# Reordering a chunked RWKV7 + MLP kernel: corner transpose ahead of an MLP piece, a second N tile, groups in pairs, weight conversions ahead of the third inverse

## The chip, the cores and the metric

One NeuronCore of a Trainium2 chip. The metric is the device time of one execution in microseconds (us). Every kernel was run four times on the chip (one of the runs with the profiler), beside runs of the kernel before on the same chip. Engine names are those of the profile: PE is the matrix engine, PEld its weight loads, DVE the vector engine, ACT the scalar engine, POOL the GpSimd engine, SP the engine that issues the DMAs.

## The reference

An RWKV7 recurrence over 768 steps for 4 batches x 8 heads with head size 40, whose output is fed as 3072 rows of 320 to an MLP with exact gelu.

```python
for t in range(S):                       # S = 768
    y[:, :, t] = einsum('bhd,bhde->bhe', rt, state)
    Sa = einsum('bhde,bhe->bhd', state, at)
    state = state * wt - einsum('bhd,bhe->bhde', Sa, bt) + einsum('bhd,bhe->bhde', vt, kt)
x = y.transpose(0, 2, 1, 3).reshape(B * S, H * D)      # 3072 x 320
h = x @ w_in                                           # 320 x 2048
out = (0.5 * h * (1 + erf(h / sqrt(2)))) @ w_out       # 2048 x 320
```

The MLP's weights arrive as 64-bit floats. The kernel loads their words and makes 32-bit floats of them on the chip.

## The kernel before

The sequence is cut into 12 chunks of 64 steps. Each chunk needs groups of small matmuls on PE (N, RV, A, M, av, X, sap, saT, QY and so on, 64 matmul records each), and the inverse of a triangular block, which is done by column steps on POOL (on DVE for chunk 0). "Corner" and "joined" put two 32-wide inverses together to a 64-wide one. The MLP of a chunk is cut into 8 pieces, four `ph` and four `po`; `fill()` puts one piece into PE's order between groups.

The corner's transpose L is issued where the corner is:

```python
def corner(c):
    t = turned_in[c]
    Tt, _ = inverses[c]
    L = work.tile([P, 2 * G * NP, BL], FP32, tag="L", name="L")
    nc.vector.transpose(L, flat(Tt)[:, :, :BL])
    N = flat(t["N"])
    J = duo("J")[:, 0].rearrange(...)
    for n in range(2 * G * NP):
        for q in range(2):
            mm(J[...], N[lo[q], n, BL:], L[lo[q], n])
    ...
```

The last two of the four `po` pieces end with a copy `os` on DVE, and each `ph` piece ends with a gelu on ACT into `gt`, a tile that also serves as scratch for the raw words of w_in at the start:

```python
def mlp(c):
    xt = xts.pop(c)
    for q in range(NF // 4):
        ph = duo("ph")...                      # 40 matmul records from xt and w_in_sb
        nc.scalar.activation(gt[:, 4 * q:4 * q + 4]..., ph, ACT.Gelu)
        yield
    po = duo("po")[:, :, :DM]
    for part in range(2):
        for g in range(G):                     # 16 matmul records from gt and w_out_sb
            ...
            if part:
                os = work.tile([P, DM], FP32, tag="os", name="os")
                nc.vector.tensor_copy(os, po[:, g])
                ...                            # stores to out
            yield
```

One conversion of words to floats. `convert(n)` advances a queue of these generators, so that the second half of one follows the first half of the next:

```python
def to_float(dst, words, eng):                 # eng: POOL for w_in, DVE for w_out
    ...
    nc.vector.tensor_scalar(power, hi, 0x7FF00000, None, ALU.bitwise_and)
    nc.scalar.activation(power, power, ACT.Relu, bias=rebias, scale=8.0)
    nc.vector.tensor_scalar(mant, hi, 0x000FFFFF, 0x00100000, ALU.bitwise_and, ALU.bitwise_or)
    yield
    nc.vector.scalar_tensor_tensor(power, hi, 0x80000000, power, ALU.bitwise_and, ALU.bitwise_or)
    if eng is nc.vector:
        ...                                    # two more operations on DVE
    else:
        nc.scalar.mul(lo_f, lo, 2.0 ** -52)
        nc.scalar.mul(mant_f, mant, 2.0 ** -20)
        eng.tensor_tensor(mant_f, mant_f, lo_f, ALU.add)
        eng.tensor_tensor(dst, mant_f, power_f, ALU.mult)
    yield
```

The start is laid by hand; on each engine the instructions stand in the order of these calls (one transpose that stood behind a copy on DVE cost 11.6 us in the loop, as b_corner below shows). The part around the third inverse (chunk 2's, on POOL), and the end of the start:

```python
    first_pieces(range(NK), 1, nc.gpsimd)      # the second half of w_in, five conversions
    ...
    make_N(2)
    run(start_inverse(2, nc.gpsimd))
    convert(1)
    fill()
    make_y2(1)
    make_M(1)
    convert(1)
    load_v(2)
    load_r(2)
    turn_k(2)
    convert(1, True)
    second_load(4, 6)
    fill()
    second_pieces((*range(NF - 2), NF - 1, NF - 2), nc.vector)
    seconds(2, (5, 2, spare_raw), (6, 0, spare_raw))
    fill()
    make_QY(1)
    outputs(1)
    ...                                        # w_out's conversions between the groups of chunk 2
```

The loop over chunks 2 to 11, cut to the part that matters:

```python
    for c in range(2, NCH):
        ...
        make_QY(c); outputs(c); pieces.append(mlp(c))
        ...
        if more2:
            turn_b(n + 1)
        fill()                                 # a po piece: its os copy is on DVE
        if more:
            corner(n)                          # L behind that os copy on DVE
        if more2:
            turn_k(n + 1); make_N(n + 1); run(start_inverse(n + 1, nc.gpsimd))
        fill()
        if more:
            joined(n)
```

## Time and profile before

| | before |
|---|---|
| time, median (range) of 4 runs | 843.96 us (840.51 to 844.67) |
| span of the profiled run | 838.1 us |
| start, to the first matmul of X(2) | 254.3 us |
| loop, from X(2) to the end | 583.8 us |
| one chunk of the loop | 56.06 us |

The page cuts the span into 40 slices; a digit is a tenth, and in the row PEclk it is the granted clock of PE. Two rows of the page of the kernel before:

```profile
PE   7236771165669999999999999999999999999997
PEclk8555595575859999999999999999999999999999
```

Up to the 12th slice PE is idle for over a fifth of each slice, in two of them for over four fifths, and often at half clock; after that it is full. So anything that shortens the first 254 us must take away waits, and anything that shortens the rest must take away work or waits of PE itself. The prediction below shows the waits.

### The profile page before, as it was taken

How to read it: one execution, taken by the hardware profiler on the slowest of the kernel's cores; microseconds unless marked ns; L12 is line 12 of the kernel's file. 1: busy time of each engine (PE TensorE's matmuls, PEld its weight loads, DVE VectorE, ACT ScalarE, POOL GpSimd, SP SyncE). 2: the span in 40 equal slices, each digit the busy share in tenths (PEclk: the TensorE clock that was granted, in tenths of full speed). 3: DMA queues.
4: the chain of work that ended last, by engine and by line, in shares of the span. 5: the costliest groups of instructions: out<-in, count | busy, mean ns of one | idle time of the engine just before them, and what ended most of it. 6: DMA issues, size and time to landing. Idle time of an engine off the chain costs nothing.

```text
span 838.1 us, 30219 instructions
## 1 busy us (share of the span) xinstructions
PE 702.7 (84%) x13646; PEld 563.3 (67%) x13646; DVE 279.1 (33%) x422; ACT 214.0 (26%) x260; POOL 315.2 (38%) x781
## 2 busy tenths in 40 slices
PE   7236771165669999999999999999999999999997
PEld 4226661054448878778788787787887877868785
DVE  3763440147542422432424324324233243211000
ACT  5002540212312412422323124223232242111010
POOL 4282336620105507418246074182461751810000
PEclk8555595575859999999999999999999999999999
DMA  9876743017617247354372473543724733020000
GB/s 132 158 156 130 147 112 89 0 40 155 142 34 140 43 82 130 60 103 80 64 135 50 84 135 55 109 77 68 129 57 76 142 55 65 4 53 10 25 9 16
DMA packets 274705, 70.27 MB, mean 84 GB/s; under 512 B 263248, under 2 KB 267856, under 8 KB 274576
## 3 DMA queue, kind: packets, MB, share of 16 engines
q1 hardware_dynamic: 274412, 68.17, 42.6%
q8 instruction: 107, 1.75, 0.9%
q14 instruction: 22, 0.18, 0.1%
q10 hardware_dynamic: 164, 0.16, 0.1%
HBM read 54.13 MB, written 10.22 MB: 77 GB/s over the span
## 4 chain that ended last, share of the span: by engine, by line
PE 73%; POOL 6%; DMA 6%; issue 5%; SPq 4%; DVE 4%; ACT 0%; POOLq 0%; DVEq 0%
PE ph L726 25%; PE po L734 24%; PE QY L100 5%; PE J L100 2%; PE N_ps L100 2%; DMA w_out_sb<-in_moe_w_in_dram 2%; PE cum L100 2%; PE M_ps L100 1%; POOL W L548 1%; POOL mant L281 1%; PE sap L100 1%; POOL tmp L546 1%; PE saT_ps L100 1%; PE X L100 1%; PE wT_ps L100 1%
## 5 line engine op out<-in xcount | busy, mean ns | idle before, releaser
L726 PE MATMUL ph<-xt,w_in_sb 64*128 64x256 f32 x1920 | 225.8, 388 | 42.2 <-ACT gt L728 29.8
L734 PE MATMUL po<-w_out_sb,gt 128*128 128x320 f32 x768 | 225.7, 448 | 9.1 <-DVE w_out_sb L277 8.0
L726 PEld LDWEIGHTS ph<-xt,w_in_sb 64*128 64x128 f32 x1920 | 185.7, 190 | 68.0 <-ACT gt L728 30.2
L734 PEld LDWEIGHTS po<-w_out_sb,gt 128*128 128x128 f32 x768 | 145.9, 195 | 72.2 <-DVE w_out_sb L277 12.4
L546 POOL TENSOR_TENSOR tmp<-W,Nb 128x126 f32<-128x126 f32 (+22 forms) x310 | 111.8, 361 | 213.2 <-DMA Nb<-N 189.7
L548 POOL TENSOR_TENSOR W<-W,tmp 128x126 f32<-128x126 f32 (+22 forms) x310 | 113.9, 368 | 24.3
L728 ACT ACTIVATE gt<-ph 128x1024 f32<-128x1024 f32 x48 | 49.1, 1024 | 232.5 <-PE ph L726 197.5
L738 DVE COPY os<-po 128x320 f32<-128x320 f32 x24 | 11.8, 492 | 152.5 <-PE po L734 152.5
L413 POOL TENSOR_TENSOR ks<-k_raw,part 128x640 f32<-128x640 f32 x10 | 21.2, 2119 | 100.5 <-ACT part L378 85.1
L100 PE MATMUL RV_ps<-rT,vT 40*64 40x64 f32 x768 | 16.4, 244 | 30.8 <-DVE rT L166 30.8
L100 PEld LDWEIGHTS RV_ps<-rT,vT 40*64 40x64 f32 x768 | 14.7, 156 | 34.5 <-issue 34.5
L686 DVE TENSOR_TENSOR xt<-QY,wpT 128x512 f32<-128x512 f32 x24 | 15.5, 686 | 65.5 <-PE QY L100 65.5
L464 DVE TENSOR_TENSOR SM<-M_ps,upper 128x1024 f32<-128x1024 f32 x12 | 14.7, 1224 | 65.7 <-PE M_ps L100 65.7
L464 DVE TENSOR_TENSOR A<-A_ps,upper 128x1024 f32<-128x1024 f32 x12 | 14.7, 1221 | 54.6 <-PE A_ps L100 54.6
L520 ACT COPY avs<-av 128x640 f32<-128x640 f32 x12 | 8.3, 692 | 90.4 <-PE av L100 51.8
L464 DVE TENSOR_TENSOR VR<-RV_ps,upper 128x1024 f32<-128x1024 f32 x12 | 14.7, 1225 | 47.7 <-PE RV_ps L100 47.7
L100 PE MATMUL J<-L,N 32*32 32x32 f32 x768 | 9.9, 204 | 23.9 <-DVE L L585 23.9
L270 ACT ACTIVATE power<-power,rebias 128x320 uint32<-128x320 uint32 (+1 forms) x26 | 16.0, 623 | 51.6 <-DVE power L269 51.6
L100 PEld LDWEIGHTS J<-L,N 32*32 32x32 f32 x768 | 8.9, 116 | 29.4 <-issue 29.4
L464 DVE TENSOR_TENSOR N<-N_ps,upper 128x1024 f32<-128x1024 f32 x12 | 14.7, 1225 | 36.0 <-PE N_ps L100 36.0
L424 DVE TENSOR_TENSOR aT<-aT,wpT 128x1024 f32<-128x1024 f32 x12 | 24.0, 2001 | 1.6 <-ACT wpT L380 0.4
L728 ACT ACT_TABLE_LOAD x10 | 12.8, 1283 | 42.6 <-PE ph L726 40.1
(133 smaller groups left out, 869.0 us busy)
## 6 DMA issues: line engine op xcount, KB each, us to landing
Nb<-N SPq DMA_DIRECT2D x22, 256.0 KB
VR<-in_v_dram SPq DMA_DIRECT2D x24, 160.0 KB
out_dram<-os SPq DMA_DIRECT2D x48, 80.0 KB
w_tile<-in_w_dram SPq DMA_DIRECT2D x22, 160.0 KB
b_raw<-in_b_dram SPq DMA_DIRECT2D x22, 160.0 KB
k_raw<-in_k_dram SPq DMA_DIRECT2D x22, 160.0 KB
v_pairs<-in_v_dram SPq DMA_DIRECT2D x48, 72.0 KB
r_pairs<-in_r_dram SPq DMA_DIRECT2D x48, 72.0 KB
```

The costliest lines, as they stand in the source:

```text
L100: nc.tensor.matmul(o, lhsT, rhs, start=first, stop=True, skip_group_check=True)
L270: nc.scalar.activation(power, power, ACT.Relu, bias=rebias, scale=8.0)
L413: nc.gpsimd.tensor_tensor(ks[:, :, :, :D], raws.pop((c, "k")), rwv, ALU.mult)
L424: nc.vector.tensor_tensor(flat_a, flat_a, wp, ALU.mult)
L464: nc.vector.tensor_tensor(to, pt, upper.unsqueeze(1).to_broadcast([P, 2 * G * NP, C]), ALU.mult)
L546: eng.tensor_tensor(t, W[:, :rows, j:j + 1].to_broadcast([P, rows, rest]), Nb[:, j:j + 1, j + 1:].to_broadcast([P, rows, rest]), ALU.mult)
L548: eng.tensor_tensor(W[:, :rows, j + 1:], W[:, :rows, j + 1:], t, ALU.add)
L686: nc.vector.tensor_tensor(xt[:, :NP, g * P:(g + 1) * P].rearrange("p i (e t) -> p i e t", e=2), Y, wp[:, g, :, :, :C], ALU.mult)
L726: nc.tensor.matmul(ph[:, x, s], w_in_sb[half(x), kt, p * P:(p + 1) * P], xt[half(x), kt], start=kt == 0, stop=kt == NK - 1)
L728: nc.scalar.activation(gt[:, 4 * q:4 * q + 4].rearrange("p (x s) t -> p x s t", x=2), ph, ACT.Gelu)
L734: nc.tensor.matmul(po[:, g], gt[:, f, g * P:(g + 1) * P], w_out_sb[:, f], start=f == 0, stop=f == NF - 1)
L738: nc.vector.tensor_copy(os, po[:, g])
```

## The change

The intent: in the loop, take the corner's transpose out of PE's way, and put two groups of matmuls into each gap between MLP pieces (which needs a second N tile, since N of the chunk after next is now written ahead of the join). In the start, have all of w_in converted ahead of the third inverse, which occupies POOL for 27 us. The core of the diff; other moves of loads and turns are cut.

```diff
@@ to_float
-        yield
+        if eng is nc.vector:
+            yield
@@ make_N
-        N = t["N"] = work.tile([P, 2, G, NP, C], FP32, tag="turned" if c == 1 else "N", name="N")
+        if c > 1 and c % 2:
+            N = work.tile([P, 4 * DM], FP32, tag="spare", name="N")[:, :2 * G * NP * C]
+            N = N.rearrange("p (j g n t) -> p j g n t", j=2, g=G, n=NP)
+        else:
+            N = work.tile([P, 2, G, NP, C], FP32, tag="turned" if c == 1 else "N", name="N")
+        t["N"] = N
@@ corner
+    def turn_corner(c):
+        L = turned_in[c]["L"] = work.tile([P, 2 * G * NP, BL], FP32, tag="L", name="L")
+        nc.vector.transpose(L, flat(inverses[c][0])[:, :, :BL])
@@ start: the third inverse
+    convert(4, True)
     run(start_inverse(2, nc.gpsimd))
-    convert(1)
+    second_load(4, 6)
+    second_load(5, 2, spare_raw)
+    second_load(6, 0, spare_raw)
     fill()
+
+    second_pieces((*range(NF - 2), NF - 1, NF - 2), nc.vector)
     make_y2(1)
     make_M(1)
-    convert(1)
+    seconds(2, (7, 14))
+    fill()
     load_v(2)
     load_r(2)
...
     make_QY(1)
     outputs(1)
+    pieces.append(mlp(1))
+    seconds(2, (8, 12), (9, 10))
     load_VR(3)
...
+    fill()                                 # the fourth ph piece, now behind QY(1)
+    turn_k(2)
     turn_v(2)
     turn_r(2)
     make_RV(2)
...
-    seconds(1, (15, 14))
+    seconds(2, (13, 2, spare_raw))
+    store_inverse(2)                       # stood further up, ahead of scale(3)
+    fetch_inverse(2)
     turn_b(3)
+    seconds(1, (14, 0, spare_raw), (15, 14))
@@ loop
+        corner(c)
         make_X(c)
         fill()
         if more2:
-            load_next(n + 1)
+            load_next(n2)
+        joined(c)
         if more:
             make_RV(n)
+        fill()
         make_sa(c)
-        fill()
         make_saT(c)
-        if more:
-            make_A(n)
         fill()
...
-        fill()
-        if more:
-            corner(n)
-        if more2:
-            turn_k(n + 1)
-            make_N(n + 1)
-            run(start_inverse(n + 1, nc.gpsimd))
+        fill()
+        if more2:
+            make_N(n2)
+            run(start_inverse(n2, nc.gpsimd))
+            turn_k(n2)
+        if more:
+            turn_corner(n)
         fill()
-        if more:
-            joined(n)
```

More of the change, by code (lines that the diff above doesn't have):

```diff
@@ L203 @@
     ahead = {n: t.rearrange("p (g h d) -> p g h d", g=G, h=H) for n, t in ahead.items()}
-    spare_raw = const.tile([P, 4 * DM], UINT32, name="spare_raw")
+    spare_raw = work.tile([P, 4 * DM], UINT32, tag="spare", name="spare_raw")
     early_a = spare_raw.bitcast(FP32).rearrange("p (n d) -> p n d", d=BW)
@@ L578 @@
     hi = [slice(q * HP + BL, (q + 1) * HP) for q in range(2)]
+    def turn_corner(c):
+        L = turned_in[c]["L"] = work.tile([P, 2 * G * NP, BL], FP32, tag="L", name="L")
+        nc.vector.transpose(L, flat(inverses[c][0])[:, :, :BL])
     def corner(c):
         t = turned_in[c]
-        Tt, _ = inverses[c]
-        L = work.tile([P, 2 * G * NP, BL], FP32, tag="L", name="L")
-        nc.vector.transpose(L, flat(Tt)[:, :, :BL])
+        if "L" not in t:
+            turn_corner(c)
+        L = t.pop("L")
         N = flat(t["N"])
@@ L799 @@
     load_VR(0)
-    load_v(0)
     spare_x = work.tile([P, NK, TB], FP32, tag="xt", name="spare_x").rearrange("p k t -> p (k t)")
@@ L807 @@
     run(start_inverse(1, nc.gpsimd, (spare_x[:, :BL * BL], spare_w[:, :nw], spare_w[:, nw:])))
+    load_v(0)
     load_r(0)
@@ L812 @@
     first_load(False, 1)
-    first_load(True, 0, early(4))
     run(inverse)
     store_inverse(0)
+    load_VR(1)
+    fetch_inverse(0)
     turn_v(0)
@@ L821 @@
     turn_k(1)
-    make_A(1, False)
-    load_VR(1)
-    fetch_inverse(0)
-    load_v(1)
-    first_load(False, 2, early(5, 4))
-    first_pieces(range(NK), 0, nc.gpsimd)
-    mask_A(1)
-    corner(0)
+    load_v(1)
+    first_load(True, 0, early(4))
+    first_pieces((0, 1), 0, nc.vector)
+    convert(2)
+    corner(0)
+    make_A(1, False)
     joined(0)
@@ L832 @@
     make_sa(0)
-    convert(1)
+    mask_A(1)
+    first_pieces((2, 3, 4), 0, nc.gpsimd)
+    make_saT(0)
     store_inverse(1)
@@ L836 @@
     load_r(1)
-    load_w(2)
-    make_saT(0)
     convert(1)
-    fetch_inverse(1)
     make_y2(0)
     make_M(0)
-    convert(1)
+    fetch_inverse(1)
+    load_w(2)
     load_a(2)
     load_kb(2)
-    logs(2)
-    first_load(False, 3)
+    convert(1)
     make_QY(0)
@@ L850 @@
     pieces.append(mlp(0))
-    first_load(True, 1, spare_raw[:, :LW])
+    first_load(False, 2, early(5, 4))
     turn_v(1)
@@ L855 @@
     turn_state()
+    first_load(False, 3)
+    first_load(True, 1, spare_raw[:, :LW])
     convert(1)
@@ L860 @@
     make_X(1)
-    convert(1)
+    logs(2)
     first_pieces(range(NK), 1, nc.gpsimd)
@@ L866 @@
     make_sa(1)
-    scale(2)
+    scale_b(2)
     turn_a(2)
     scale_a(2)
-    convert(1)
     make_saT(1)
     turn_b(2)
+    scale_k(2)
+    for f, at in enumerate((14, 12, 10, 8)):
+        second_load(f, at)
     convert(1)
     fill()
-    for f, at in enumerate((14, 12, 10, 8)):
-        second_load(f, at)
     make_N(2)
+    convert(4, True)
     run(start_inverse(2, nc.gpsimd))
-    convert(1)
+    second_load(4, 6)
+    second_load(5, 2, spare_raw)
+    second_load(6, 0, spare_raw)
     fill()
+    second_pieces((*range(NF - 2), NF - 1, NF - 2), nc.vector)
     make_y2(1)
     make_M(1)
-    convert(1)
+    seconds(2, (7, 14))
+    fill()
     load_v(2)
     load_r(2)
-    turn_k(2)
-    convert(1, True)
-    second_load(4, 6)
-    fill()
-    second_pieces((*range(NF - 2), NF - 1, NF - 2), nc.vector)
-    seconds(2, (5, 2, spare_raw), (6, 0, spare_raw))
-    fill()
     make_QY(1)
     outputs(1)
+    pieces.append(mlp(1))
+    seconds(2, (8, 12), (9, 10))
     load_VR(3)
-    pieces.append(mlp(1))
-    seconds(3, (7, 14), (8, 12))
-    load_w(3)
-    load_a(3)
-    load_kb(3)
+    fill()
+    turn_k(2)
     turn_v(2)
@@ L905 @@
     make_A(2)
+    load_w(3)
+    load_a(3)
+    load_kb(3)
+    seconds(3)
+    seconds(2, (10, 2, spare_raw), (11, 0, spare_raw), (12, 14))
+    fill()
     make_av(2)
-    seconds(2, (9, 10))
+    logs(3)
     load_v(3)
     load_r(3)
-    seconds(2, (10, 2, spare_raw), (11, 0, spare_raw))
-    fill()
-    logs(3)
-    seconds(2, (12, 14))
     sums(3)
-    store_inverse(2)
-    fetch_inverse(2)
     scale(3)
@@ L919 @@
     scale_a(3)
-    seconds(2, (13, 2, spare_raw), (14, 0, spare_raw))
+    seconds(2)
     turn_state()
     fill()
-    seconds(1, (15, 14))
+    seconds(2, (13, 2, spare_raw))
+    store_inverse(2)
+    fetch_inverse(2)
     turn_b(3)
+    seconds(1, (14, 0, spare_raw), (15, 14))
     seconds(2, last=True)
     fill()
-    corner(2)
-    turns_b(3)
     make_N(3)
     run(start_inverse(3, nc.gpsimd))
+    turns_b(3)
+    turn_corner(2)
     fill()
-    joined(2)
     for c in range(2, NCH):
-        n = c + 1
-        more, more2 = n < NCH, n + 1 < NCH
+        n, n2 = c + 1, c + 2
+        more, more2 = n < NCH, n2 < NCH
+        corner(c)
         make_X(c)
@@ L939 @@
         if more2:
-            load_next(n + 1)
+            load_next(n2)
+        joined(c)
         if more:
             make_RV(n)
+        fill()
         make_sa(c)
-        fill()
         make_saT(c)
-        if more:
-            make_A(n)
         fill()
@@ L952 @@
         if more2:
-            logs(n + 1)
+            logs(n2)
         make_QY(c)
@@ L956 @@
         pieces.append(mlp(c))
+        fill()
         if more2:
-            load_VR(n + 1)
-            turn_a(n + 1)
-            turn_v(n + 1)
-            turn_r(n + 1)
-        fill()
+            load_VR(n2)
+            sums(n2)
         if more:
-            make_av(n)
+            make_A(n)
+            turn_state()
         if more2:
-            sums(n + 1)
-            scale(n + 1)
-            scale_a(n + 1)
-        if more:
-            turn_state()
+            scale(n2)
+            turn_a(n2)
+            scale_a(n2)
         fill()
@@ L974 @@
             fetch_inverse(n)
+            make_av(n)
         if more2:
-            turn_b(n + 1)
+            turn_b(n2)
+            turn_v(n2)
+            turn_r(n2)
         fill()
+        if more2:
+            make_N(n2)
+            run(start_inverse(n2, nc.gpsimd))
+            turn_k(n2)
         if more:
-            corner(n)
-        if more2:
-            turn_k(n + 1)
-            make_N(n + 1)
-            run(start_inverse(n + 1, nc.gpsimd))
+            turn_corner(n)
         fill()
-        if more:
-            joined(n)
     fill(1000)
```

## The prediction

> **What bounds the kernel now.** I read the page first (its slices show two regimes), then the busy time in stretches, then PE's waits and timeline in each regime, then whatever those waits named.
>
> Busy time by stretches (start:end; us; PE, PEld, DVE, ACT, POOL with instruction counts; PE clock; DMA share; GB/s):
>
> ```profile
> 100.00:125.00 25.00, 19.79 (x375) 16.57 (x377) 10.55 (x17) 14.27 (x20) 9.87 (x10) 0.85 0.40 106
> 125.00:150.00 25.00, 3.47 (x124) 2.93 (x113) 1.23 (x1) 0.00 (x0) 16.36 (x44) 0.56 0.32 74
> 150.00:175.00 25.00, 7.06 (x28) 4.29 (x30) 6.53 (x11) 6.57 (x10) 15.96 (x27) 0.50 0.08 27
> ...
> 325.00:350.00 25.00, 25.00 (x502) 20.39 (x499) 10.85 (x13) 8.57 (x9) 17.55 (x41) 1.00 0.31 61
> 350.00:375.00 25.00, 23.71 (x488) 18.76 (x488) 7.07 (x9) 5.28 (x6) 2.89 (x11) 1.00 0.52 96
> ```
>
> From 254 us to the end PE is full at clock 1.00; one chunk takes 56.06 us (RV starts at 259.98, 316.06, 372.12 in the chain). Every second or third stretch lacks exactly 1.29 us. Before 254 PE is a third to a half idle, often at half clock. So the run is a start of 254 us bound by waits, and a loop of 584 us bound by PE. PE's waits in the start, and then in the loop (total, times, longest):
>
> ```profile
> PE RV_ps L100 <- DVE rT L166: 30.8, 2, 19.7
> PE ph L726 <- ACT gt L728: 29.8, 1, 29.8
> PE ph L726 <- POOL w_in_sb L282: 12.4, 4, 4.1
> ...
> PE po L734 <- DVE w_out_sb L277: 8.0, 6, 2.8
> ```
>
> ```profile
> PE J L100 <- DVE L L585: 11.6, 9, 1.3
> PE po L734 <- DVE os L738: 1.2, 2, 0.6
> ```
>
> *The long wait.* "ACT gt" is only the last link. The timelines of PE, POOL and ACT around it:
>
> ```profile
> 128.00 1.81 PE L388 MATMUL kT_ps<-ident,ks 128*128 128x128 f32 x8 [1.35 <-DVE SM L464]
> 159.61 2.08 PE L726 MATMUL ph<-xt,w_in_sb 64*128 64x256 f32 x8 [29.80 <-ACT gt L728]
> ```
>
> ```profile
> 157.23 1.27 POOL L281 TENSOR_TENSOR mant<-mant,gt 128x512 f32<-128x512 f32 x1
> 158.58 1.27 POOL L282 TENSOR_TENSOR w_in_sb<-mant,power 128x512 f32<-128x512 f32 x1
> ```
>
> ```profile
> 158.54 1.02 ACT L728 ACTIVATE gt<-ph 128x1024 f32<-128x1024 f32 x1 [34.95 <-POOL mant L281]
> ```
>
> The third inverse occupies POOL from 130.27 to 157.2. The conversions of the second half of w_in stand behind it; the second gelu overwrites gt, which still holds their raw words, so it waits too, and PE waits for its bank. POOL then needs until 172.4 for the four conversions left, and ph trickles with them.
>
> *The short wait.* In DVE's order the corner's transpose L stands behind the output copy os, which waits for the end of the po piece just ahead of the corner on PE:
>
> ```profile
> 357.23 0.49 DVE L738 COPY os<-po 128x320 f32<-128x320 f32 x1 [6.22 <-PE po L734]
> 357.64 0.70 DVE L585 STREAM_TRANSPOSE L<-Tt 128x512 f32<-128x512 f32 x1
> ```
>
> 0.49 + 0.70 and two hand-overs make the 1.29 us, nine times.
>
> [...]
> 1. [...]the w_in wait of 4.07 us at 114.30 is followed by 24 matmuls in 4.72 us, where 40 take 4.59 us in the loop.
> 2. [...]L and the gelu above are held by what stands ahead of them.
> 3. [...]a po piece takes 4.50 us start to next start between tiled groups (338.67 to 343.17), 4.31 beside transposes (347.54 to 351.85): about 0.19 us for one stay in the full-array mode.
> 4. [...]the two mask operations of a w_out conversion took 1.39 and 1.42 us at 169.86 while POOL converted, 0.32 each at 187.33 with POOL idle.
>
> **The change part by part.** I laid out each engine's new order with the durations above; starts are in us of the span.
>
> *Loop.* The transpose L goes ahead of the last po piece, so it is done 4 us before PE asks for it; the second N tile only lets the new N be written while the corner still reads the old one. Removed: 9 x 1.29 = 11.6 us. Pairing groups adds and removes no matmul. Full-array stays per chunk fall from five (po; cum; tn-po-nT-po; kT; po) to four (po-cum; tn-po; nT-po; kT-po): 1 x 0.19 x 9 = 1.7 us. Joined(2) moves inside the loop's account: +0.7. Net -12.6 us. New waits I looked for: with two groups and a piece per gap a bank of the four comes back about 4.5 us after its last writer, evictions take 0.4 to 1.3 us; tn needs cum's bank (exp, 0.7 us) two groups later; av needs A's mask a whole piece later. All hidden.
>
> *Start, to the first ph piece: about nothing.* Moving v loads behind the second inverse's load starts that inverse some 3 us sooner on POOL, but slows DVE's inverse beside it; one and a half conversions go to DVE ahead of the first corner (6 or 7 operations, about 4.5 us). L(0) stays near 62.9, the first QY ends near 83 (81.2 before), the second corner near 88 (87.9 before). The first ph piece starts at 108 as before.
>
> *First ph piece: gain 6 us.* Its five w_in conversions are now done by 96, so the 4.07 us wait and the half clock go: end 112.7, not 118.95; M of chunk 1 ends near 120.3, not 126.6.
>
> *The third inverse.* Four conversions remain after N(2). Each is 2.55 us on POOL, fed through DVE and ACT, and with the two buffers of power and mant: POOL runs from 117.4 to about 129.5. The gelu of the second ph piece stands behind the last one on ACT, so the third ph piece gets its bank at about 128 (half clock: 6.5 us, to 134.5). QY(1) ends at 137.5, not 184.3: **47 us earlier**. The inverse itself runs from 129 to 157, as now, but nothing needs it before 178.
>
> *What is given back.* From QY(1) to the loop's first X it was 184.3 to 254.3, 70 us. Now the fourth ph piece stands inside (+4.5); v and r of chunk 2 load only after spare_raw is free (near 130), so RV comes at about 147; the w_out conversions, 1.93 us each (187.33 to 189.25), begin beside the inverse[...]. Five of them (to 162), av, log and cum (168), po (175), then the loads of the last three w_out rows, of which two stand in the queue behind the inverse's store and fetch (about 9 us, as at 216.48 to 224.7): third po piece done near 200; N, kT, po and J (1.9 + 1.9 + 6.3 + 1.0, as after 241.2) put X(2) at about 212. So 74.5 us, not 70: the start gains 254.3 - 212 = **42 us**.
>
> Sum: 844.3 - 42 - 12.6 = 789.7, say **790 us**.
>
> **The rivals.**
> (a) *The start's gain is taken back by the w_out chain.* For: DVE, ACT and the one DMA queue make each w_out row in turn and PE waited 8.0 us for them; the raw rows share few slots. Against: of 70 us there, much was work and waits that simply move. If the loads slip another 15 us: about 805.
> (b) *Only the loop counts*, if some DMA sets the time of QY(1): the second half of w_in is now loaded later, after xt. For: 2 MB at about 160 GB/s take 12.5 us. Against: they land near 106 to 109, and the first is needed at 109. If QY(1) moved only 20 us: about 815.
> (c) *The loop gets a new wait* from the pairing, of 1 us per chunk: about 800. Against: PE's only waits in the loop are those above.
> (d) *The start goes better*: [...]RV earlier: about 778.
>
> **Range and chances.** (a) and (c) are likelier than (d), so 790 already carries some contention; the hand-laid start can be 15 us off either way: 772 to 808. Within 2% would need under 17 us, when the loop alone gives 12 and the POOL block 30: 0.03. Slower needs a stall not seen here: 0.01.
>
> **What would show it.** Right: no PE wait for L in the loop, period near 54.6 us; no PE wait over 10 us between 105 and 140; POOL's third inverse after the last w_in conversion, near 129; QY(1) end near 137; X(2) near 212. Wrong: a period still near 56 or a new wait for a PSUM bank in the loop; the ph wait turned into an equal wait for w_out, v/r or DMA between 137 and 212.

The sum stays as recorded, 844.3 - 42 - 12.6 = 789.7, said as 790 us. Inside the 42 one term is cut: about 3 us, an estimate without a source, that the w_out conversions beside the inverse were to lose. "Five of them (to 162)" contains it. Item 4 has such operations longer beside POOL; why, the traces don't show.

- The 0.19 us for one stay (groups whose matmuls the trace gives as 128\*128, between smaller tiles) is the estimate from the two times in item 3. What costs it is not shown.
- The 6.5 us for a `ph` piece at half clock are an estimate too: the first piece lost 1.97 us (24 matmuls in 4.72 us, where the loop's pace gives 2.75), and 4.59 + 1.97 is 6.56. The clock records have half clock there, from 114.6 to 118.0 us.
- "About 160 GB/s" is an estimate from the page, which has up to 158 GB/s in the first four slices of the kernel before.
- That an inverse on POOL slows the one on DVE: column steps of 128x56 took DVE 0.22 us each at 29.82 and 30.07 with POOL idle, 0.40 and 0.44 at 46.08 and 46.52 with POOL at its own inverse. The cause is not shown.

## The result

| | before | after |
|---|---|---|
| time, median (range) of 4 runs | 843.96 us (840.51 to 844.67) | 805.43 us (801.70 to 806.65) |
| span of the profiled run | 838.1 us | 802.8 us |
| start, to X(2) | 254.3 us | 220.4 us |
| loop, from X(2) to the end | 583.8 us | 582.4 us |

The ratio is 0.9544 (95% interval 0.9501 to 0.9586). Here and below, a ratio is the mean time of one kernel's runs over that of the other's of the same rounds, so not quite the ratio of the medians. The time lies inside the range that was predicted, near its upper end; 15 us are missing from the predicted gain of 54. The table says where: the start gained 34 us and not 42, and the loop hardly gained at all. (The profiled run of the kernel before took 839.78 us, less than the four in the table, so the two profiles differ by 35.3 us and the medians by 38.5.) The same two rows of the page of the kernel after:

```profile
PE   7326675467699999999999999999999999999997
PEclk8555677867699999999999999999999999999999
```

**The start.** Busy time by stretches of the kernel after, with the columns that the prediction explains:

```profile
100.00:125.00 25.00, 19.54 (x416) 16.22 (x418) 9.92 (x14) 11.56 (x16) 5.98 (x5) 0.83 0.71 171
125.00:150.00 25.00, 16.54 (x288) 14.27 (x280) 13.11 (x17) 6.88 (x10) 21.29 (x40) 0.80 0.48 115
150.00:175.00 25.00, 10.32 (x142) 6.49 (x142) 21.81 (x44) 5.75 (x9) 12.93 (x33) 0.69 0.66 139
...
550.00:575.00 25.00, 23.82 (x582) 20.65 (x580) 4.79 (x5) 6.25 (x8) 17.23 (x46) 0.93 0.69 130
```

Between 125 and 150 us PE now works 16.5 us, where it worked 3.5: the block behind the third inverse is gone. From 150 on DVE is the full engine (21.8 of 25 us); it converts w_out. The last row is in the loop, where PE should be full at clock 1.00, and is not. PE's waits in the first 240 us of the kernel after, largest first:

```profile
PE RV_ps L100 <- DVE rT L166: 31.6, 2, 21.0
PE po L745 <- DVE w_out_sb L278: 16.0, 9, 6.9
...
PE ph L737 <- POOL mant L282: 8.3, 1, 8.3
PE saT_ps L100 <- issue: 5.5, 1, 5.5
```

The 29.8 us for the gelu have become 8.3. The wait for w_out doubled, from 8.0 to 16.0. And 5.5 us are put down to "issue", that is, to nothing the profile shows. These lines of PE's timeline place them (start, length, what, count, and in brackets the idle time ahead of it):

```profile
109.16 1.44 PE L100 MATMUL saT_ps<-Tt,part 64*64 64x64 f32 x38 [5.46 <-issue]
...
112.43 5.99 PE L737 MATMUL ph<-xt,w_in_sb 64*128 64x256 f32 x40
118.34 1.16 PE L100 MATMUL N_ps<-aT,nT 40*64 40x64 f32 x64
...
134.39 6.94 PE L737 MATMUL ph<-xt,w_in_sb 64*128 64x256 f32 x40 [8.35 <-POOL mant L282]
...
160.49 1.99 PE L100 MATMUL RV_ps<-rT,vT 40*64 40x64 f32 x64 [10.61 <-DVE rT L166]
...
206.76 1.43 PE L745 MATMUL po<-w_out_sb,gt 128*128 128x320 f32 x2 [6.93 <-DVE w_out_sb L278]
```

The first `ph` piece starts at 112.4 us, behind the stop, N of chunk 2 at 118.3, the third `ph` piece at 134.4, and RV of chunk 2 at 160.5. A reason for the last is on DVE:

```profile
148.91 1.29 DVE L697 TENSOR_TENSOR xt<-QY,wpT 128x512 f32<-128x512 f32 x2 [10.70 <-PE ph L737]
```

There is one tile xt. The output of chunk 1 may not be written into it before the fourth `ph` piece of chunk 0 has read it. The change puts that piece behind QY(1), so DVE, with everything behind it in its order, stands for 10.7 us.

The 6.93 us before the third `po` piece are on the one DMA queue. Its issues there:

```profile
193.14 0.35 SPq L343 DMA_DIRECT2D spare_raw<-in_moe_w_out_dram  x1
193.59 1.28 SPq L567 DMA_DIRECT2D inv<-W  x2
197.91 1.91 SPq L577 DMA_DIRECT2D Tt<-inv  x4
...
200.88 0.45 SPq L343 DMA_DIRECT2D spare_raw<-in_moe_w_out_dram  x1
```

The last w_out rows, issued at 200.88 and 201.38, stand behind the inverse's store and fetch.

**The loop.** PE's waits in the kernel after from 220 us to the end, all but one of 0.4 us:

```profile
PE RV_ps L100 <- issue: 4.3, 3, 1.6
PE po L745 <- DVE os L749: 1.7, 3, 0.6
```

J no longer waits for L. But from one QY to the next it takes 54.83, 54.49, 54.49, 54.53, then 56.26, 57.59, 58.44, 55.74 us (the last period, without a chunk ahead to prepare, is 49.30). Four periods are as predicted; the next four are 1.3 to 4.0 us too long, 10.1 us together. What PE does in one of them:

```profile
558.35 0.34 PE L100 MATMUL RV_ps<-rT,vT 40*64 40x64 f32 x8 [1.18 <-issue]
558.62 6.28 PE L737 MATMUL ph<-xt,w_in_sb 64*128 64x256 f32 x40
```

PE stops with 8 matmuls of RV left, for 1.18 us and no releaser that the profile names. The `ph` piece after it then takes 6.28 us in place of 4.59. The clock records of the trace have half clock from 559.0 to 562.4 us, and again from 617.1 to 620.5 after a stop of 1.64 us with 13 matmuls left; after the stop of 1.44 us at 502 there is none. The three stops, a smaller one of 0.4 us, and the two slow pieces (1.69 and 1.63 us) make 8.0 of the 10.1 us. Laid group by group against the period from 348.55 us, the three stops cost 1.75, 1.41 and 1.95 us, some 0.3 us more each than the idle time, and two `ph` pieces ahead of the join take 0.35 and 1.05 us longer (the second holds the smaller stop); with the two slow pieces that accounts for the 10.1 us.

**What could stop PE with no releaser.** The page's DMA queues have this row:

```profile
q8 instruction: 107, 1.75, 1.0%
```

107 transfers of 1.75 MB are 16 KB each. PE has 13,646 matmuls and as many weight loads in the page, and 225 other instructions in the trace: 27,517, or 257 for each transfer. That the step is 256 is read from the places of the stops (under a_fewer_loads below); I call 256 instructions, taken as what one transfer brings, a portion. The join and RV, which stand side by side here, are 64 + 64 matmul records with as many weight loads: 256 instructions, and PE passes them in about 1.8 us (499.19 to 501.02). The suspicion, then: PE runs through a portion faster than the next one can be had. The times of the transfers in the trace, against PE's stops:

| PE stopped | instruction transfer | PE went on |
|---|---|---|
| saT, 103.70 | 106.28 to 107.61 | 109.16 |
| RV, 501.02 | 499.51 to 500.99 | 502.46 |
| RV, 557.17 | 555.38 to 556.71 | 558.35 |
| RV, 615.09 | 614.16 to 615.21 | 616.73 |

PE goes on 1.47 to 1.64 us after the transfer has ended. At 103.7 the transfer itself came late, at a time when the loads of w_in held the DMA engines (share 0.71); that they delayed it is not shown.

### The profile page after: what moved, and what is told of

Read it like the earlier page. It is cut to its first block, busy times and chain, and to the rows that moved or that the text cites. A ratio compares the mean times of both kernels' runs of the same rounds, so it can differ in the third digit from the quotient of the medians.

```text
span 802.8 us, 30317 instructions
## 1 busy us (share of the span) xinstructions
PE 702.6 (88%) x13646; PEld 564.4 (70%) x13646; DVE 282.3 (35%) x426; ACT 213.7 (27%) x256; POOL 311.4 (39%) x777
## 3 DMA queue, kind: packets, MB, share of 16 engines
q8 instruction: 107, 1.75, 1.0%
## 4 chain that ended last, share of the span: by engine, by line
PE 80%; DVE 5%; SPq 5%; DMA 5%; issue 3%; ACT 1%; POOL 0%; DVEq 0%; POOLq 0%; ACTq 0%
PE ph L737 27%; PE po L745 25%; PE QY L100 5%; PE J L100 2%; PE RV_ps L100 2%; PE N_ps L100 2%; PE cum L100 2%; PE sap L100 2%; PE av L100 2%; PE saT_ps L100 2%; PE A_ps L100 2%; PE wT_ps L100 2%; PE nT_ps L389 1%; PE tn_ps L389 1%; PE kT_ps L389 1%
## 5 line engine op out<-in xcount | busy, mean ns | idle before, releaser
L745 PE MATMUL po<-w_out_sb,gt 128*128 128x320 f32 x768 | 222.9, 443 | 17.9 <-DVE w_out_sb L278 16.0
L737 PEld LDWEIGHTS ph<-xt,w_in_sb 64*128 64x128 f32 x1920 | 188.2, 192 | 33.6 <-POOL mant L282 8.5
L745 PEld LDWEIGHTS po<-w_out_sb,gt 128*128 128x128 f32 x768 | 143.4, 193 | 80.6 <-DVE w_out_sb L278 22.5
L555 POOL TENSOR_TENSOR W<-W,tmp 128x126 f32<-128x126 f32 (+22 forms) x310 | 116.2, 375 | 24.3
L414 POOL TENSOR_TENSOR ks<-k_raw,part 128x640 f32<-128x640 f32 x10 | 16.1, 1614 | 62.1 <-ACT part L379 47.3
L543 POOL MEMSET W<- 128x512 f32 x10 | 5.3, 530 | 69.6 <-DMA inv<-W 69.6
L619 DVE COPY Tt<-J 32x512 f32<-32x512 f32 x12 | 8.3, 689 | 68.0 <-ACT Tt L619 67.9
L443 ACT COPY kT<-kT_ps 128x1024 f32<-128x1024 f32 x12 | 12.1, 1012 | 58.0 <-PE kT_ps L389 58.0
L646 DVE COPY SM<-sap 128x640 f32<-128x640 f32 x12 | 9.9, 825 | 44.4 <-PE sap L100 44.4
L100 PE MATMUL QY<-SM,nb 64*64 64x104 f32 x768 | 21.3, 263 | 3.4 <-DVE SM L465 3.4
```

Source lines behind the costliest of these rows:

```text
L100: nc.tensor.matmul(o, lhsT, rhs, start=first, stop=True, skip_group_check=True)
L414: nc.gpsimd.tensor_tensor(ks[:, :, :, :D], raws.pop((c, "k")), rwv, ALU.mult)
L443: nc.scalar.copy(kT, flip(by_pair(t["ks"]), "kT_ps"))
L555: eng.tensor_tensor(W[:, :rows, j + 1:], W[:, :rows, j + 1:], t, ALU.add)
L737: nc.tensor.matmul(ph[:, x, s], w_in_sb[half(x), kt, p * P:(p + 1) * P], xt[half(x), kt], start=kt == 0, stop=kt == NK - 1)
L745: nc.tensor.matmul(po[:, g], gt[:, f, g * P:(g + 1) * P], w_out_sb[:, f], start=f == 0, stop=f == NF - 1)
```

## The experiments

Theory A: the loop's stops come from the loads of the next chunk, which stand near RV. Theory B: they come from where the portions of instructions begin. (The expectations call a transfer a fetch, and the begin of a portion a 256-instruction boundary.) For the start the question was which edit brings the gain, and which terms give it back.

Expected and measured, for each kernel against the kernel before, in rounds of the same chip:

| label | median us (range) | ratio (95%) | X(2) us | period us |
|---|---|---|---|---|
| b_corner | 831.85 (825.32 to 832.79) | 0.9868 (0.9822 to 0.9914) | 259.1 | 54.71, once 54.89 |
| loop_only | 830.80 (827.17 to 833.86) | 0.9858 (0.9819 to 0.9897) | 250.2 | 54.6 to 57.9 |
| start_only | 807.75 (806.60 to 809.57) | 0.9601 (0.9570 to 0.9631) | 222.3 | 56.06, once 57.68 |
| b_conv_first | 806.03 (804.78 to 809.89) | 0.9586 (0.9550 to 0.9622) | 221.1 | 56.06, once 56.21 |
| a_loads_later | 806.90 (803.86 to 808.46) | 0.9560 (0.9520 to 0.9599) | 220.0 | 54.6 to 58.1 |
| a_shift | 798.26 (796.12 to 801.27) | 0.9464 (0.9420 to 0.9509) | 226.1 | 54.5 to 55.1 |
| a_conv_early | 804.46 (800.00 to 807.49) | 0.9519 (0.9462 to 0.9577) | 221.5 | 54.5 to 59.5 |
| a_store_early | 800.90 (798.30 to 802.13) | 0.9489 (0.9451 to 0.9527) | 214.3 | 54.5 to 58.4 |
| a_shift16 | 799.60 (795.69 to 801.40) | 0.9510 (0.9462 to 0.9558) | 217.9 | 54.5 to 56.3 |
| a_fewer_loads | 802.99 (799.40 to 806.96) | 0.9558 (0.9500 to 0.9616) | 220.7 | 54.5 to 58.2 |
| b_both | 794.31 (791.30 to 794.70) | 0.9445 (0.9402 to 0.9489) | 220.2 | 54.71 |
| a_best | 786.73 (784.63 to 788.97) | 0.9358 (0.9305 to 0.9412) | 214.8 | 54.49 |

X(2) and the period are from the profiled run, the period without the last one. All results were correct, but for a_fewer_loads, which is wrong.

### b_corner: the kernel before, with the transpose L ahead of the po piece, and nothing else

```diff
         if more2:
             turn_b(n + 1)
+        if more:
+            turn_corner(n)
         fill()
         if more:
             corner(n)
```

> The kernel before, with one edit: the corner's transpose L is issued on DVE ahead of the po piece that precedes the corner (no second N tile, no pairing). Theory (L only stood behind the output copy): PE's nine waits of 1.29 us in the loop go, period 56.06 to 54.77 us, span 838.1 to about 826.5, time about 832. Rival (the wait is the fetch of the inverse, or the pairing and the second N tile are needed): period stays near 56 us, time near 843.

The period falls to 54.71 us. PE's waits in its loop:

```profile
PE po L738 <- DVE os L742: 1.2, 2, 0.6
PE J L100 <- DVE L L582: 0.2, 1, 0.2
```

The 11.6 us are gone by moving one DVE instruction, with one N tile and without pairs. No stop of the kind above falls into this loop. The pairs of the whole change can then be worth no more than 54.71 - 54.49 = 0.22 us per chunk.

### loop_only and start_only: one half of the change each

loop_only is the start of the kernel before and the new loop, start_only the reverse. Where they meet, the last calls of the start have the form that the loop needs:

```diff
 # loop_only: the end of the start before
-    corner(2)
-    turns_b(3)
     make_N(3)
     run(start_inverse(3, nc.gpsimd))
+    turns_b(3)
+    turn_corner(2)
     fill()
-    joined(2)
```

> The start of before with the loop of after. Theory A (the loop by itself is worth 11.6 + 1.7 - 0.7 us, and the 10 us lost in after's chunks 7 to 9 come from where PE's 256-instruction fetches fall, which the start decides only by its count of instructions, almost the same): the same late stalls show, loop about as long as in after, time 838 to 843. Theory B (the late stalls belong to the shifted start, not to the loop): no stalls, period 54.5 throughout, time about 831.

> The start of after with the loop of before. Theory (start gains 254.3 - 220.4 = 34 us, the loop of before keeps its 1.29 us per chunk and has no fetch stalls): span about 804, time about 810. Rival (the two parts are not additive, the start's gain only shows with the new loop): time over 818.

The start alone brings nearly all that the whole change brings; the loop alone 1.4%. If the two gains simply added, the product of the ratios, 0.9601 x 0.9858 = 0.9465, should be the ratio of the whole change; it is 0.9544. So the parts don't add, by some 6.7 us, of which the intervals of the three ratios leave about 5.4 us either way open (an estimate from them). start_only came as expected (807.75 against about 810), but for one period of 57.68 us: there PE's ordinary wait of 1.29 us for L was followed by half clock from 608.84 to 612.25 us; after the eight others in this loop it was not. For loop_only the expected time, 838 to 843 us, was missed (830.8). In loop_only the stops are there too, but elsewhere: in saT with 11 matmuls left at 264.9 us (0.76 us), in RV with 3 and 9 left at 591.4 and 648.6 us (1.44 and 0.88 us), and none of over 0.6 us at 500 to 560. The loop's code is the same, only the number of instructions ahead of it differs: for theory B (the expectation above calls it Theory A).

### b_conv_first: the kernel before, with the w_in conversions ahead of the third inverse

```diff
     make_N(2)
+    convert(3, True)
     run(start_inverse(2, nc.gpsimd))
-    convert(1)
     fill()
     make_y2(1)
     make_M(1)
-    convert(1)
     load_v(2)
     load_r(2)
     turn_k(2)
-    convert(1, True)
     second_load(4, 6)
     fill()
```

> The kernel before, with one edit: the remaining w_in conversions ahead of the third inverse on POOL (and so the gelu no longer waits for it). Theory (POOL's order is the start's cause, the rest of the start's reorder gives little or takes back): the first X of chunk 2 comes 25 to 40 us earlier than 254.3, time 805 to 818. Rival (it needs whole conversions, DVE's share and the moved loads): gain under 20 us, time over 824.

One moved block brings X(2) to 221.1 us, as the whole rewritten start does (220.4). The loop still has its old wait, as it must:

```profile
PE J L100 <- DVE L L585: 11.6, 9, 1.3
```

So the loads, conversions and turns that the change also moved in the start bring nothing on balance: the rewritten start has QY(1) 7.4 us sooner (141.3 against 148.7) and has lost this again by X(2). A difference of a few us could not be seen here, as X(2) comes between 217.9 and 226.1 us in the kernels with the start of the kernel after whose own edit should leave it alone.

### a_loads_later: the kernel after, with the loads of the next chunk one piece later

```diff
         fill()
-        if more2:
-            load_next(n2)
         joined(c)
         if more:
             make_RV(n)
         fill()
+        if more2:
+            load_next(n2)
```

> The kernel after, with the loads of chunk c+2 in the loop issued one MLP piece later (after the second gap instead of after the first). Theory (in chunks 7 to 9 a boundary of PE's 256-instruction fetch falls at the end of the gap J2 and RV, and the fetch stands behind the small-packet loads of a): the three stalls of 1.2 to 1.6 us in RV and the half-clock pieces behind them go; loop 582 to about 572 us, time about 795; stalls may show up in the next gap instead. Rival (the clock is throttled late in the run, or the stall has nothing to do with the loads): loop stays near 582, time 803 to 807.

A miss for theory A. The stops stay at the same matmuls: with 2, 8 and 13 left, of 0.97, 1.75 and 0.81 us. One of them:

```profile
560.61 0.40 PE L100 MATMUL RV_ps<-rT,vT 40*64 40x64 f32 x8 [1.75 <-issue]
```

### a_shift: the kernel after, with 124 more PE instructions in the first microseconds

```diff
-    for n in range(3):
+    for n in range(2):
         mm(pt[:, n % 2], w_in_sb[:, 0, :P], w_in_sb[:, 0, :512])
+    for n in range(32):
+        mm(pt[:64, 0, :64], w_in_sb[:64, 0, :64], w_in_sb[:64, 0, :64])
```

The added matmuls are tiny, and their results are not used. They do nothing but move every later instruction to another place in its portion.

> The kernel after, with the PE stream shifted by 124 instructions: one warm-up matmul less, 32 tiny ones more at the very start. Theory (stalls sit where a 256-instruction boundary meets a dense gap under load): the stalls leave RV of chunks 7 to 9 and show in other chunks or gaps, or vanish; the clock dips of 0.93 move with them. Rival (late throttle): the dips stay at 550 to 625 us whatever the shift. Time 793 to 808, the place decides, not the time.

The RV stops are gone, and the loop takes 573.4 us and not 582.4, although its code is the same to the letter. That the profiled run is only 3 us faster (the median 7) comes from the start: X(2) is at 226.1, with two stops, of 3.17 and 3.55 us, near 103 and 111 us, where the kernel after has one of 5.46.

### a_shift16: 64 more instructions

```diff
     make_A(0, False)
+    pt = duo("pad")
+    for n in range(16):
+        mm(pt[:64, 0, :64], w_in_sb[:64, 0, :64], w_in_sb[:64, 0, :64])
```

The same idea with 16 tiny matmuls in an idle stretch of the start. Half the shift lets theory B say where the stops should be: the kernel after, in its successive iterations, has them with 2, 8 and 13 matmuls left, so some five and a half more each time, and 32 records of shift should bring them into iterations 2 to 4.

> The kernel after, with 16 tiny matmuls (64 PE instructions) added in the start where PE idles. In after the stalls of RV leave 2, 8 and 13 of its 64 matmul records behind in chunks 7, 8 and 9, so a 256-instruction boundary lies there and moves some 5.5 records earlier per chunk. Theory (the place of the boundary decides): 64 instructions more move it 32 records earlier, so the stall in RV now comes in chunks 2 to 4 (about 6, 12 and 17 records left), none in RV of chunks 7 to 9. Rival (late throttle or the absolute time): RV stalls stay in chunks 7 to 9. Time 795 to 807.

PE's timeline has them there:

```profile
227.08 0.48 PE L100 MATMUL RV_ps<-rT,vT 40*64 40x64 f32 x6 [1.78 <-issue]
...
285.99 0.45 PE L100 MATMUL RV_ps<-rT,vT 40*64 40x64 f32 x12 [1.14 <-issue]
...
342.22 0.50 PE L100 MATMUL RV_ps<-rT,vT 40*64 40x64 f32 x17 [0.74 <-issue]
```

And there are none in iterations 7 to 9. This is the strongest evidence for theory B: the place of the stop was predicted to the iteration and the matmul from a count of instructions.

### a_fewer_loads: the loads of a, v and r left out for chunks 9 to 11 (wrong)

```diff
-        if more2:
+        if more2 and n2 < 9:
             load_next(n2)
+        elif more2:
+            load_w(n2)
+            load_kb(n2)
+            for name in ("a", "v", "r"):
+                raws[n2, name] = paired[name]
```

This asks whether the instructions come late because of the chunk's small-packet loads. Its results are wrong (relative error 0.705), which does not matter for the question.

> The kernel after, with the loads of a, v and r left out in chunks 7, 8 and 9 (their tiles keep an older chunk's data: the result is wrong on purpose). Theory A (the fetch comes late because it stands among data transfers): the stalls of RV in chunks 7 to 9 go, loop 582 to about 573 us, time about 796. Theory B (the fetch is late whatever the load, since 256 instructions pass in under 2 us there): the stalls stay, time about 804.

The stops stay, with 2, 8 and 13 left, of 2.13, 1.60 and 1.16 us:

```profile
561.68 0.34 PE L100 MATMUL RV_ps<-rT,vT 40*64 40x64 f32 x8 [1.60 <-issue]
```

So those loads aren't needed for the stop. Three things can be counted in the traces of all fourteen kernels, in which I find 46 stops of PE of over 0.6 us under "issue":

- *Where.* Counted in PE's own order, with weight loads and semaphore instructions, the instruction at which PE stopped has a number that leaves 192 to 195 when divided by 256, all 46 times. The three RV stops of the kernel after are at 17,089, 19,394 and 21,697. So every stop is at the same place of a stretch of 256, which I take as the begin of a new portion.
- *When it ends.* PE went on 1.30 to 1.74 us after the end of the last instruction transfer, and 2.3 to 3.1 us after its begin, all 46 times. In the loops no two such transfers begin less than 3.24 us apart. In the kernel after a transfer took 0.88 to 1.79 us.
- *What it needs.* Of the portions passed after 225 us, 760 took PE 6 us or more, and none of them ended in a stop of over 0.3 us; of the 459 that took less, 38 did. So all 38 of these stops came after a quickly passed portion, and most quickly passed portions had none.

The last point also bounds what may be said of the change. The kernel before has the join beside X, 256 instructions in 1.8 us as well (365.78 to 367.54), and in its loop portions passed in 1.83 to 2.6 us without a stop. In the loops of the five kernels with the old order no stop of over 0.3 us fell; of the nine with the new order seven have some. But the portions were shifted on purpose in the new order alone. That the pairs as such cause stops is therefore not shown, and not excluded; what is shown is that the stops come at portion boundaries and move with them. How far the portion was ahead each time, which may decide between the 38 and the others, stays open. This part is read from the traces after the fact; no run changed the transfer itself.

### a_conv_early: the kernel after, with four w_out conversions ahead of the outputs of chunk 1

```diff
     make_QY(1)
+    seconds(2, (8, 12), (9, 10))
     outputs(1)
     pieces.append(mlp(1))
-    seconds(2, (8, 12), (9, 10))
```

This uses DVE's idle 10.7 us for conversions that otherwise stand behind it. (`seconds(2, ...)` advances two conversions and issues two loads.)

> The kernel after, with the two w_out conversions that follow outputs(1) issued ahead of it on DVE. Theory (DVE idles 10.7 us because xt(1) must wait for the fourth ph piece, which after put behind QY(1), and two conversions then stand between it and vT, rT): RV of chunk 2 comes at about 155 instead of 160.5, the first X of chunk 2 3 to 6 us earlier, time 800 to 803. Rival (the loads of r or the third po piece set the time anyway): X(2) within 1 us of 220.4, time about 805.

Largely a miss. From the start of the third `ph` piece to RV it takes 20.0 us in place of 26.1, and the wait before RV shrank from 10.61 to 5.03, but from QY(1) to X(2) only 2.5 us remain of it (76.6 against 79.1), and the time can't tell them from nothing. The w_out conversions further on set the pace there. In this profile QY(1) itself came at 145.0 and not 141.3, after a stop of 3.41 us in saT near 111 us.

### a_store_early: the kernel after, with the inverse's store and fetch ahead of the load of row 13

```diff
+    store_inverse(2)
+    fetch_inverse(2)
     seconds(2)
     turn_state()
     fill()
     seconds(2, (13, 2, spare_raw))
-    store_inverse(2)
-    fetch_inverse(2)
     turn_b(3)
```

> The kernel after, with the store and fetch of the third inverse issued ahead of the load of w_out row 13, where the queue stood idle 10 us. Theory (rows 14 and 15 wait behind the store and fetch): PE's wait of 6.9 us in the third po piece falls to about 2 us, X(2) about 5 us earlier, time about 800. Rival (the rows wait for their slots, or DVE's conversions set the pace): X(2) within 1.5 us of 220.4, time about 805.

A hit: the wait of 6.93 us is gone, and 2.84 is the longest one left in that piece:

```profile
201.06 1.44 PE L745 MATMUL po<-w_out_sb,gt 128*128 128x320 f32 x2 [2.84 <-DVE w_out_sb L278]
```

X(2) comes at 214.3 us, 6 us sooner; but QY(1), which stands ahead of the edit, already came at 139.2 and not 141.3. From QY(1) to X(2) it takes 75.2 us in place of 79.1, so about 4 us are the edit's. The loop has the RV stops of the kernel after, with 2, 7 and 13 matmuls left, longer (1.98, 1.66 and 1.73 us), and two more in saT (1.08 and 0.84); it takes 586.1 us and not 582.4.

### b_both: the kernel before with the two small edits, L ahead and conversions ahead

```diff
 # the edits of b_corner and b_conv_first together, on the kernel before:
+    convert(3, True)                       # ahead of the third inverse; three convert(1) behind it removed
     run(start_inverse(2, nc.gpsimd))
...
+        if more:
+            turn_corner(n)                 # ahead of the po piece
         fill()
         if more:
             corner(n)
```

> The kernel before with two small edits only: L ahead of the po piece, and the w_in conversions ahead of the third inverse. Theory (start and loop gains add, and the old order of groups meets no fetch stalls): 806 - 11 = 795. Rival (the gains don't add, or fetch stalls come with any shorter period): 800 to 806.

PE's waits in its loop, all of them:

```profile
PE po L738 <- DVE os L742: 1.2, 2, 0.6
PE J L100 <- DVE L L582: 0.8, 1, 0.8
```

794.31 us: with two moved blocks it is some 8 us faster than the whole change (0.9445 against 0.9544 of the kernel before; the medians, from two chips, differ by 11). The gains add: 0.9868 x 0.9586 = 0.9459, measured 0.9445. Its period is 54.71 us throughout, and it has no stop in the loop, in this alignment of its portions.

### a_best: the kernel after with a_store_early, a_conv_early, and 31 tiny matmuls in the idle start

```diff
     make_A(0, False)
+    pt = duo("pad")
+    for n in range(31):
+        mm(pt[:64, 0, :64], w_in_sb[:64, 0, :64], w_in_sb[:64, 0, :64])
...
     make_QY(1)
+    seconds(2, (8, 12), (9, 10))           # ahead of outputs(1), not behind it
     outputs(1)
...
+    store_inverse(2)                       # ahead of the load of row 13
+    fetch_inverse(2)
     seconds(2)
```

> The kernel after, with the store and fetch of the third inverse earlier, the two conversions ahead of outputs(1), and 31 tiny matmuls (124 PE instructions) added where PE idles in the start. Theory (the three are independent: about -5, -2, -9): 788 to 793, no RV stall in the loop, X(2) near 213. Rival (start gains absorb each other): 795 to 798.

The only PE wait left in its loop:

```profile
PE po L745 <- DVE os L749: 1.8, 3, 0.6
```

786.73 us, the fastest of all, 1.3 us below the expected range. Its loop takes 571.5 us from X(2) to the end; the prediction had 571.2 (583.8 - 12.6). The number of 31 is meant for this order alone, and no other was tried with these edits: any added or removed PE instruction ahead of the loop moves the portions again.

## Why the prediction was right or wrong

The predicted 790 us came out as 805.4, inside the range of 772 to 808, and "faster by over 2%" was right. The range held partly by luck: it allowed 15 us for the hand-laid start, which missed by 8, and most of the other loss is in the loop, from a cause that it had no allowance for. Step by step:

- **What bounds the kernel: right.** b_conv_first and b_corner take the two waits that it named away, one by one, and get 4.1% and 1.3%.
- **The loop, -12.6 us: right in mechanism, given back by a wait that it did not have.** No wait for L, no wait for a PSUM bank; the undisturbed period is 54.49 us against the 54.6 expected, and a_best gets the whole of it. The kernel after got 1.4 us, since 10 us went into stops where a portion begins and the half clock after two of them. Rival (c) put a new wait into every chunk, from the pairing, and took PE's waits as a reason against it. It was right about the time lost ("about 800"), but not about the wait: it is another one, in four chunks of eight, at the boundaries of portions. The profile of the kernel before did show such transfers (107) and two such stops, in its start, but I did not read those rows.
- **The 1.7 us for fewer full-array stays: right in size.** a_best's period is 0.22 us shorter than b_both's, near the estimate of 0.19 per chunk; the orders differ in more than this, so the split is not shown.
- **First `ph` piece, gain of 6 us: failed.** Its w_in words were there, as the step had it: the wait of 4.07 us is gone. But the stop of 5.46 us in saT, which the step did not have, let the piece start at 112.4 and not 108, half clock (to 115.3 us) made it 5.99 us long, and it ended at 118.4 and not 112.7. The words of the second half of w_in landed near 114, where the prediction had 106 to 109: it counted 2 MB, and the loads are 2.62 MB, which the DMA engines moved between 97.8 and 115.4 us.
- **The third inverse: right, a term mis-sized.** POOL starts it behind the last w_in conversion, as said, but that ended at 135.6 and not 129.5. This is the delay of the step before, handed on: the four conversions stand behind N of chunk 2 in DVE's order, and N began at 118.3 and not near 112.7. In the nine kernels with this start the last conversion ends 17.25 to 17.98 us after N begins (the prediction had 16.8), whenever that is. Single operations did take longer beside each other, as foreseen (the mask on DVE took 1.51 us at 129.93 while POOL converted, and 0.41 just before), but that is within the 0.5 us of difference. In a_shift16, without a stop in its start, N began at 115.4 and QY(1) ended at 140.5; what holds back these 3 us is open. So the third `ph` piece came at 134.4 and not 128, and QY(1) ended near 144.3 and not 137.5: 40 us earlier, not 47.
- **What is given back, 74.5 us from the end of QY(1) to X(2): right in sum, 76, but by luck.** RV was expected at 147 and came at 160.5: the step counted the fourth `ph` piece as 4.5 us of PE, and missed that the one tile xt makes DVE wait for it. The DMA queue's 9 us were seen in advance; a_store_early shows that about 4 of them were on the path. The third `po` piece was done at 212.5, not near 200: 68 us after QY(1) and not 62.5. The groups behind it made up for most of this: they took 7.9 us and not 12, as the step counted them at half clock and the clock records have full clock from 214.3 us.
- **Sum:** start 34 and not 42 us, loop 1.4 and not 12.6. Together 35.3 us between the two profiles, in place of 54.6.

Open are how far the next portion must be ahead for PE to pass without a stop, and why the stops in the start differ from one kernel to the next (0 to 5.5 us for one stop); there they move X(2) by a few microseconds either way, in the kernels before and after alike.

## What to carry to other kernels

Look past the last releaser of a wait to what stands ahead of it in the order of the same engine: here moving one transpose (11.6 us), and one block of conversions (X(2) at 221.1 us in place of 254.3), brought all of the gain that a rewrite of start and loop did. After a reorder of many short matmuls, read the period chunk by chunk and look for "issue" waits: this loop, its other waits gone, still lost 10 us to stops where a portion begins and to what followed them, and with 64 more instructions ahead of it the stops moved from iterations 7 to 9 to iterations 2 to 4. And before a piece is moved behind its successor, ask which single tile it reads.
